# A new job list, new store gates and new planner constants for a convolution followed by a token mixer

## The chip, the cores and the metric

The kernel runs on one core of a Trainium2 chip. The metric is the device time of an execution in microseconds (us), as the median of several runs. The profile is that of a single execution: its span runs from the first to the last instruction, and its own time is a little longer than the span.

## The reference, cut to what matters

```python
# x: 8 x 4224 x 192; weight: 8 x 7; w_q, w_k: 192 x 64; w_out: 192 x 192; all float32
w = softmax(weight)                                  # over the 7 taps, one row per head of 24 channels
y[b, s, head h] = sum_k w[h, k] * x_padded[b, s + k, head h]   # causal, six zeros ahead
wq, wk = y @ w_q, y @ w_k
mixed  = (scale * wq @ wk.T) @ y                     # per batch, scale = 1 / 8
out    = relu(mixed) @ w_out
```

The kernel uses that `wq (wk^T y) = y w_q (w_k^T (y^T y))`. Per batch it forms the 192 x 192 matrix `y^T y`, multiplies it by `w_k` into a 64 x 192 matrix M, and never holds the 4224 x 4224 weights between tokens.

## The kernel before, in words

A batch of 4224 tokens is split into two halves of 2112, and a half into 18 chunks of 122 tokens; a chunk is loaded with the six tokens ahead of it, on 128 partitions, and becomes bf16 in the load. Five batches of x fit in `xw`. The loads of a batch come in two parts (x4.0 is the first part of batch 4, x4.1 the second; batch 1 has four parts and batch 0 eight), all issued from POOL. `y` holds two batches, `qt` two batches, `zt` three blocks of z, and `o_sb` eight blocks of output. PSUM has eight banks: bank 7 keeps the sum of `y^T y`, and banks 0 to 6 go round among the other jobs.

All work is cut into jobs, one letter each in the string `ORDER`:

| letter | job | PE work | evicted or done by |
|---|---|---|---|
| Y | convolution of a group of chunks and heads by a band matrix (L510, L544) | 2 to 8 matmuls, mostly 2 of 128x432 | ACT or DVE to `y` |
| D | copy of the first 64 columns of `y` behind its last, so that windows of 128 wrap | none | DVE, from batch 2 on POOL too |
| T | transpose of three chunks into `yb` (L971) | none | DVE |
| G | one chunk's share of `y^T y` (L644) | 6 matmuls of 128x64 | none |
| E | `y^T y` to `gs` | none | ACT or DVE |
| M | two jobs by turns: a transpose of parts of `gs` into `gt` (L670, L671), and M (L684) | 2 or 6 small matmuls | ACT or DVE to `gt`, `m_sb` |
| Q | half a batch of `w_q^T y^T`, in tiles of 32 rows and 64 columns, on four banks (L614) | 48 matmuls of 32x288 | ACT and DVE to `qt` |
| Z | 512 tokens of a half by 128 columns of `relu(M^T q)` (L720) | 1 matmul of 128x512 | ACT or DVE to `zt` |
| O | output of 512 tokens of both halves in two jobs (L763, L765) | 6 matmuls | ACT or DVE to `o_sb`, then a store from SP |
| A | two Z and one O fused (`fused`): the two Z and O's last part run side by side in tiles of 64 rows (L1127, L1135), then O's other part (L1143) | 2 + 4 + 4 matmuls | as Z and O |
| H, W | zeros ahead of a batch; copies of weights within SBUF | none | DVE, ACT |
| h | names the four banks that the next Q will use and keeps other jobs off them | none | none |

The string is read once while the kernel is built. Each letter takes the next job of its own stream, so the order within a stream is fixed, and the string sets how the streams interleave. PE runs in just this order. For each eviction a planner (`empty`, `pick`, `place`, `fused`) takes the engine that its cost table says will be done first, and the bank that it says will be free first; for that it keeps times of every engine (`COST`, `SWITCH`), of the landing of loads and stores (`flow`, with a rate and latencies in `CLOCK`), and of the fetching of PE's instructions (`stall`, with `CLOCK["fetch"]`: a block of 256 instructions is asked for when the one before it is begun). Where PE would be idle before `CLOCK["fill"]`, it puts in small matmuls on zeros (L1002). None of these times is in the built program: only the orders, engines, banks and fillers that follow from them. The waits of the program are semaphores that come from the data alone.

Stores leave SP in the order of the O jobs; block n is number 5 b + i (i = 4 is the small rest of a batch). `GATES` maps a block to a part of x: the store of this block, and with it all stores behind it on SP, waits until that part has landed. From 4 on the part's number is 2 b + part, so that 8 is x4.0 and 15 is x7.1. A block's slot in `o_sb` is n mod 8, so its eviction waits for the store of block n - 8 to have landed. A load into `xw` waits for the convolutions of the batch five before, and is issued on POOL behind the job D of the batch three before.

Of the kernel before, what the change touches and what calls it, by code (L numbers as in the profile page):

```python
# [11 lines left out]


GATES = {
    0: 8, 3: 9, 5: 10, 10: 12, 15: 14,
}


ORDER = (
    "YYYDYDYDYGTDGGGGYDYYDGTGYYDTGDGGTYTWGGGGGHQGGGTEYYMYDYWMQZZDZZZYYGGZYTGGDGAOTGOT"  # L20
    "YGZZGDOHQGTGYGGYZODOZGYGZGYYGTGGEYYGDMYGGGMTTOGHGAZGYGYYOGTYGGZGZGZQOTGTGYGGYZOG"
    "EDZZYZhGOTGHTMGGDQTMOGZZOYZGZGTZOYTGGZYGGQZGTOQGTZOYYGDZZGZGTYYOGGOEYYGGMOZDHATO"
    "GYOMGZZTGYGGTZOQGZGDOTYGZOOGAZGYGZGZTTGYGQZGOGEAZOGTTGYGMYYGGGGMODhQGZHOGAGGTYYT"
    "GGZOTGQZYGDTGYYOGOGEZZYGDGAMGYTZGGATZOYOHGZGGGTYMQGOZYZGTGYZGATGTGYGZQOOGTAZOGEY"
    "DYGGGYGGGTMAMYOOZZZGGGZDQOTZGOGAOGZTGTGAGGGQGZEOZOMZOZMOZOTZZZOOZOZOQZOZZZOOZZZO"
    "ZOOOO"
)


CLOCK = {  # L30
    "x0": (5.0, 7.5, 9.0, 8.1, 10.2, 12.0, 13.1, 13.8), "band": 6.5, "wq": 14.0, "wk": 16.0,
    "wo": 20.5, "fill": 24.0,
    "dma": (377e3, 13.2, 1.6, {"x": 2.2, "o": 1.2}), "fetch": (64, 256, 5.5, 3.5, 120.0),
}


# [135 lines left out]
def bass_lightweight_conv__then__hypermixer_token_mlp_kernel(  # L172
# [84 lines left out]
    xg = [[P.group(f"x{b}_{g}") for g in range(len(GROUPS[b]))] for b in range(B)]  # L257
# [52 lines left out]
    for g in range(2):  # L310
# [3 lines left out]
            lambda e, g=g, at=(g * HALF + (1 - g) * CW - 6) * D: e.dma_start(  # L314
                staged[g].rearrange("p (c d) -> p c d", d=D),
                bass.AP(x_t, at, [[D, 128], [CW * D, 5], [1, D]]),
            ),
# [104 lines left out]
    band = []  # L422
    for q, eng in enumerate(("act", "dve", "dve", "dve")):
        x0, x1 = (6 if q == 0 else 0), (CW - 90 if q == 3 else 38)
# [37 lines left out]
    wq = [pool(lambda e: e.tensor_copy(WQ[:, :, :], WSQ[:, :, :]), [wl[0]], 0.55)]  # L462
# [143 lines left out]
    def job_q(b, g):  # L606
        def pe(e, bk):
            for j in range(6):
                for i in range(4):
                    r = slice(32 * i, 32 * i + 32)  # L610
                    for h in range(2):
                        c = D * h + 64 * (j // 2) + j % 2
                        rhs = YB[r, g, :, c : c + 63 : 2]
                        last = e.matmul(PS[64 * h : 64 * h + 64, bk + i, 0:288], WQ[r, j, :], rhs,  # L614
                                        start=j == 0, stop=j == 5, skip_group_check=True)
            return last

        evacs = []
        for i0, i1 in ((0, 2), (2, 3), (3, 4)):
            w = 32 if i0 < 3 else CW - 96  # L620

            def make(bk, i0=i0, i1=i1, w=w):
                o = bass.AP(QT, (b % 2) * QW + 9 * CW * g + 32 * i0,
                            [[2 * QW, 128], [32, i1 - i0], [CW, 9], [1, w]])
                i = PS[:, bk + i0 : bk + i1, 0:288].rearrange("p n (c t) -> p n c t", t=32)
                return [(o, i[:, :, :, 0:w])]

            evacs.append((make, ("Q", b, g, i0), (i1 - i0) * 9 * w, "copy"))
        return Job(
            ("Q", b, g), 4, pe, [288] * 6,  # L630
            reads=["wq"] + [("TD", b, 3 * g + k) for k in range(3)],
            after=zdone(b - 2), evacs=evacs, mode="Q",
        )
# [235 lines left out]
    x_at = {}  # L869
# [31 lines left out]

    def land(b, part):
        def f(t):
            x_at[id(xg[b][part])] = t - (b == 1) * (1.0 - 0.8 * (part == 2))
            return x_at[id(xg[b][part])]
        return f

# [72 lines left out]
        return (e.mul(o, i, scale) if eng == "act"  # L980
                else e.tensor_scalar(o, i, scale, None, op0=ALU.mult))

    FIRST, BLOCK, AWAY, NEAR, CALM = CLOCK["fetch"]
    code = [FIRST + 2 * (16 + 1 + 20), 0.0, 0.0]

    def stall(words, t, us):
        at, got = code[0], code[1:]
        to, late = at + words, 0.0
        edge = (at // BLOCK + 1) * BLOCK
        while edge <= to:  # L990
            when = t + us * (edge - at) / words + late
            ok = got[1]
            late += max(0.0, ok - when)
            when = max(ok, when)
            got = [when, when + (AWAY if when < CALM else NEAR)]
            edge += BLOCK
        return late, [to] + got

# [102 lines left out]
    def fused(n):  # L1101
        zs = streams["Z"][head["Z"] : head["Z"] + 2]
        os_ = streams["O"][head["O"] : head["O"] + n]
        b, i = zs[0].name[1:3]
        assert zs[0].name[2:] == (i, 0) and i < 4 and all(j.name[2] < 4 for j in os_)
        at, used, deps, late, t = [], [], [], [], free["pe"]
        for j in (*os_, *zs):
# [3 lines left out]
            t = max(t, free_at + SEE)  # L1111
        for k in used:
            deps += banks[k][1]
        for j in (*zs, *os_):
# [3 lines left out]
            t = max([t] + [o.end + SEE for r in j.reads for o in got(r)])  # L1118
# [27 lines left out]

        pops = []
        for fn, need, m, us, words in (
            (tails, deps, "R", 0.2183 + 0.17 * n, 4 + 8 * n), (heads, late, "F", 0.33 * n, 8 * n),
        ):  # L1150
            o = P.op("pe", fn, need)
            o.start = max(t, free["pe"]) + SWITCH.get((mode[0], m), 0.0)
            mode[0] = m
            wait, code[:] = stall(words, o.start, us)
            total[0] += wait
            o.end = free["pe"] = o.start + us + wait
            o.name = ("R" if m == "R" else "O",) + os_[0].name[1:] + (n,)
            pops.append(o)
# [55 lines left out]
```

## Time and profile before

| | |
|---|---|
| median of 3 runs | 159.13 us (158.52 to 160.15) |
| profiled execution | 158.52 us, span 156.4 us |
| granted TensorE clock | 0.996 |
| PE busy | 137.2 us, 88% of the span |
| ACT busy | 128.4 us, 82% |
| DVE busy | 120.1 us, 77% |
| POOL busy | 58.4 us, 37% |
| HBM read and written | 27.86 MB and 25.95 MB |

Busy time is a share of the whole span, and the span has a start without input and an end in which stores land. A line of groups gives the line, engine, operation, tiles and shape, then the count, the busy time and the mean of one, then the idle time just before them and what ended it. The chain goes from the last instruction back to what released each step; "issue" there is time in which an engine waited for nothing that the profile shows. A window's row has the length, then for each engine its busy time and count, then the granted clock, the DMA share (it can pass 1, since packets overlap on an engine) and the GB/s. The GB/s count a load at its bf16 size, half of what it reads.

### The profile page before, as it was taken

The page shows a single profiled execution, that of the slowest core. Times are in us where ns is not written, and L with a number is a line of the kernel's source. Part 1 is how long each engine was busy: PE and PEld are TensorE (multiplying, and loading weights), DVE is VectorE, ACT ScalarE, POOL GpSimd, SP SyncE. Part 2 cuts the span into 40 slices and gives each one's busy share as a digit, 9 for nine tenths or more (in the row PEclk, how much of TensorE's full clock was granted, in tenths as well). Part 3 has the DMA queues.
Part 4 walks back from the last instruction along what each step waited for, and adds up shares of the span by engine and source line. Part 5 has one row for each costly group of instructions (what it writes and reads, how often), then busy time and mean ns, then how long its engine had stood idle before and what let it go on. Part 6 is the DMA issues. An engine that isn't in the chain of part 4 may idle for free.

```text
span 156.4 us, 5628 instructions
## 1 busy us (share of the span) xinstructions
PE 137.2 (88%) x2431; PEld 101.0 (65%) x2456; DVE 120.1 (77%) x239; ACT 128.4 (82%) x213; POOL 58.4 (37%) x76
## 2 busy tenths in 40 slices
PE   6789758989999999999999999999597999998940
PEld 1367546767777776777777877677374777775720
DVE  6778767949987986888988959899496888795810
ACT  5568559979998899988989988898497888998950
POOL 7999899895764803444200202020020200000000
PEclk9999999999999999999999999999999999999998
DMA  3999999999999999999999999999998556599896
GB/s 100 262 197 182 189 187 187 194 189 193 191 192 192 271 339 340 227 198 341 340 292 192 277 343 337 218 253 394 381 401 323 221 203 235 204 370 395 286 387 225
DMA packets 48441, 40.83 MB, mean 261 GB/s; under 512 B 37281, under 2 KB 40481, under 8 KB 48417
## 3 DMA queue, kind: packets, MB, share of 16 engines
q0 software_dynamic: 36384, 13.35, 72.1%
q1 hardware_dynamic: 12032, 27.14, 47.7%
q8 instruction: 19, 0.31, 0.7%
q14 instruction: 6, 0.04, 0.1%
HBM read 27.86 MB, written 25.95 MB: 344 GB/s over the span
## 4 chain that ended last, share of the span: by engine, by line
PE 72%; POOL 13%; issue 5%; DVE 4%; ACT 2%; ACTq 0%; POOLq 0%
PE ps L644 15%; PE ps L544 12%; PE ps L763 11%; PE ps L765 9%; PE ps L614 8%; POOL xw L280 7%; PE ps L720 6%; PE ps L1143 3%; PE ps L1127 3%; POOL wk L352 1%; PE ps L1135 1%; ACT o_sb L975 1%; PE ps L510 1%; DVE zt L979 1%; POOL xw L297 1%
## 5 line engine op out<-in xcount | busy, mean ns | idle before, releaser
L975 ACT COPY o_sb<-ps 128x768 f32<-128x768 f32 (+1 forms) x61 | 47.2, 787 | 4.7 <-PE ps L765 3.7
L975 ACT CAST y<-ps 128x864 bf16<-128x864 f32 (+6 forms) x47 | 38.1, 833 | 7.8 <-PE ps L544 4.0
L644 PEld LDWEIGHTS ps<-y 128*128 128x128 bf16 (+1 forms) x864 | 35.5, 98 | 12.0 <-issue 2.5
L644 PE MATMUL ps<-y 128*128 128x64 bf16 (+1 forms) x864 | 40.4, 193 | 1.9 <-issue 0.8
L979 DVE TENSOR_SCALAR zt<-ps 128x512 bf16<-128x512 f32 x44 | 29.4, 680 | 8.9 <-PE ps L720 4.4
L975 POOL COPY y<-y 128x1152 bf16<-128x1152 bf16 x11 | 12.6, 1144 | 62.7 <-ACT y L975 41.8
L971 DVE STREAM_TRANSPOSE yb<-y 128x576 int32<-128x576 int32 x48 | 35.6, 758 | 0.1
L763 PE MATMUL ps<-wo,zt 128*128 128x192 bf16 x204 | 33.7, 247 | 1.9 <-ACT o_sb L975 1.2
L765 PE MATMUL ps<-wo,zt 128*128 128x384 bf16 x102 | 33.2, 326 | 0.0
L280 POOL DMA_DIRECT2D xw<-in_x_dram x35 | 32.3, 936 | 2.0 <-POOL xw L439 1.1
L978 ACT ACTIVATE zt<-ps 128x512 bf16<-128x512 f32 x52 | 30.3, 604 | 1.5 <-PE ps L1135 1.1
L763 PEld LDWEIGHTS ps<-wo,zt 128*128 128x128 bf16 x204 | 21.2, 114 | 8.4 <-ACT o_sb L975 1.6
L544 PE MATMUL ps<-xw,band 128*128 128x432 bf16 x96 | 23.9, 346 | 2.2 <-issue 1.8
L975 DVE CAST y<-ps 128x864 bf16<-128x864 f32 (+2 forms) x21 | 21.5, 1026 | 3.9 <-PE ps L544 2.5
L975 DVE CAST qt<-ps 128x288 bf16<-128x288 f32 (+1 forms) x32 | 12.2, 421 | 8.4 <-PE ps L614 8.3
L720 PE MATMUL ps<-qt,m_sb 128*128 128x512 bf16 x45 | 15.3, 380 | 1.8 <-ACT m_sb L980 1.7
L614 PE MATMUL ps<-yb,wq 32*64 32x288 bf16 x768 | 15.7, 284 | 1.0 <-ACT y L975 0.5
L975 ACT CAST qt<-ps 128x576 bf16<-128x576 f32 x16 | 10.2, 640 | 4.4 <-PE ps L614 3.7
L614 PEld LDWEIGHTS ps<-yb,wq 32*64 32x64 bf16 x768 | 10.6, 102 | 2.9 <-issue 1.3
L765 PEld LDWEIGHTS ps<-wo,zt 128*128 128x128 bf16 x102 | 11.6, 113 | 0.0
L544 PEld LDWEIGHTS ps<-xw,band 128*128 128x128 bf16 x96 | 7.4, 98 | 6.1 <-issue 1.9
L510 PE MATMUL ps<-xw,band 128*128 128x120 bf16 (+4 forms) x96 | 8.3, 226 | 2.3 <-DMA xw<-in_x_dram 1.0
(79 smaller groups left out, 121.4 us busy)
## 6 DMA issues: line engine op xcount, KB each, us to landing
out_dram<-o_sb SPq DMA_DIRECT2D x31, 768.0 KB, 7.4
xw<-in_x_dram POOLq DMA_DIRECT2D x14, 432.0 KB, 15.9
xw<-in_x_dram POOLq DMA_DIRECT2D x14, 384.0 KB, 16.9
o_sb<-in_x_dram SPq DMA_DIRECT2D x2, 480.0 KB, 4.5
out_dram<-o_sb SPq DMA_DIRECT2D x16, 48.0 KB, 6.0
out_dram<-o_sb SPq DMA_DIRECT2D x2, 384.0 KB, 3.2
xw<-in_x_dram POOLq DMA_DIRECT2D x2, 240.0 KB, 6.4
xw<-in_x_dram POOLq DMA_DIRECT2D x1, 288.0 KB, 6.9
```

Of the source, the lines that this page charges most:

```text
L280: return e.dma_start(XW[lo:hi, b % NX, half, c : c + n, :], bass.AP(x_t, at, [[D, hi - lo], [CW * D, n], [1, D]]),)
L510: last = e.matmul(PS[:, bk + j // per, at : at + w], BAND[:, h, :], XW[:, b % NX, half, c0:c1, GRP * h : GRP * h + GRP], start=True, stop= ...
L544: last = e.matmul(PS[:, k + j, 0 : 48 * n].rearrange("p (c h d) -> p h c d", h=2, d=GRP), BAND[:, h, :], rhs, start=True, stop=True,)
L614: last = e.matmul(PS[64 * h : 64 * h + 64, bk + i, 0:288], WQ[r, j, :], rhs, start=j == 0, stop=j == 5, skip_group_check=True)
L644: last = e.matmul(PS[:, 7, 64 * k : 64 * k + 64], y[:, 64 * k : 64 * k + 128], y[:, 64 * k : 64 * k + 64], start=c + h + k == 0, stop=c == ...
L720: return e.matmul(PS[:, bk, :], m[:, parts[k] : parts[k] + 128], q, start=True, stop=True)
L763: e.matmul(o[:, 192 * h : 192 * h + 192], z[:, h, cols], WO1[:, :], start=h == 0, stop=False, **kw)
L765: last = e.matmul(o[:, 0:384], z[:, 2, cols], WO2[:, :], start=False, stop=True, **kw)
L971: return e.transpose(o, i)
L975: return e.copy(o, i) if eng == "act" else e.tensor_copy(o, i)
L978: return e.activation(o, i, AF.Relu)
L979: return e.tensor_scalar(o, i, 0.0, None, op0=ALU.max)
```

## The change

The string `ORDER` is replaced, as are the gates and the constants of the planner. The functions keep what they do.

- The number of fused pairs (A) goes from 13 to 3, so Z goes from 78 to 98 letters and O from 59 to 69. The letter h goes from 2 to 5. All other letters keep their number.
- Store 0 waits for x5.0 in place of x4.0; store 8 for x5.1, store 11 for x6.1 and store 18 for x7.1. Before, stores 3, 5, 10 and 15 waited for x4.1, x5.0, x6.0 and x7.0.
- The planner's landing times of the first loads and of `w_out` shift by 0.1 to 2 us. Its time to fetch a block is 7.0 us before 98 us, 8.0 before 121 and 4.8 after, in place of 5.5 before 120 and 3.5 after. A matmul of Q is taken as 292 columns in place of 288, a fused pair as 0.02 us longer.

Counted by form, ACT gets 3 evictions of 128x768 to `o_sb`, 3 of y and one each of `gs` and the small `o_sb` more, 3 of `zt`, both of `gt`, and the five copies of `wk` and `wo` fewer. DVE gets 3 of `zt`, 2 of `gt` and the five copies more, and 3 of `o_sb` and 3 of y fewer. One D moves from DVE to POOL.

```diff
 GATES = {
-    0: 8, 3: 9, 5: 10, 10: 12, 15: 14,
+    0: 10, 8: 11, 11: 13, 18: 15,
 }

 ORDER = (
-    "YYYDYDYDYGTDGGGGYDYYDGTGYYDTGDGGTYTWGGGGGHQGGGTEYYMYDYWMQZZDZZZYYGGZYTGGDGAOTGOT"
-    "YGZZGDOHQGTGYGGYZODOZGYGZGYYGTGGEYYGDMYGGGMTTOGHGAZGYGYYOGTYGGZGZGZQOTGTGYGGYZOG"
-    "EDZZYZhGOTGHTMGGDQTMOGZZOYZGZGTZOYTGGZYGGQZGTOQGTZOYYGDZZGZGTYYOGGOEYYGGMOZDHATO"
-    "GYOMGZZTGYGGTZOQGZGDOTYGZOOGAZGYGZGZTTGYGQZGOGEAZOGTTGYGMYYGGGGMODhQGZHOGAGGTYYT"
-    "GGZOTGQZYGDTGYYOGOGEZZYGDGAMGYTZGGATZOYOHGZGGGTYMQGOZYZGTGYZGATGTGYGZQOOGTAZOGEY"
-    "DYGGGYGGGTMAMYOOZZZGGGZDQOTZGOGAOGZTGTGAGGGQGZEOZOMZOZMOZOTZZZOOZOZOQZOZZZOOZZZO"
-    "ZOOOO"
+    "YYYDYYDYDGGGGYYDTDGYTYGDGTGDTYQYDGGGGGGHTYGTGGGYWYEMDhMQZDZZYZYWYGTDTYGZGZGOYGOO"
+    "DZTTTGGOGGhZhGZGHQGGYZYYGZYGGGDYGOETGGZYTMGTZOGHMGOYYGZGYQGYGDZYTGZZTGYGZGGYGQDG"
+    "ZOTZGYGZOETOOGZYGHGMTZDYQGZTYGOOGOTMOZGGZZTZTYDGhZhQYGGHZYGTYGYGZGOTYZOYGGGEYZDO"
+    "ZOMGOZGGQOZYZGMOTGGYZTYOZGOZZGOGGGDGYGOTGZYYGTGZGGEQOGZGHZOGMGYTOTYZGZGZDYODGMZZ"
+    "TZGGGQGYGZGOZOTOZZZGYYGTGOZOZYOZGGZOTHQZEOTZYYDGYGGZGGTQOGGMZZOYMOGYDGYZOOTZZZOZ"
+    "ZOGGZGGYTGYGOOZTGYOGGEZOGMZZYGDZMGTTOQGTZOGGTGATGOOGGQGZZZTGQZGOAZTOGGGTGGEAMOMZ"
+    "ZOZZZOZOOZOQZOZZZOOZZZOZOOOO"
 )

 CLOCK = {
-    "x0": (5.0, 7.5, 9.0, 8.1, 10.2, 12.0, 13.1, 13.8), "band": 6.5, "wq": 14.0, "wk": 16.0,
-    "wo": 20.5, "fill": 24.0,
-    "dma": (377e3, 13.2, 1.6, {"x": 2.2, "o": 1.2}), "fetch": (64, 256, 5.5, 3.5, 120.0),
+    "x0": (5.0, 7.5, 8.9, 8.1, 10.0, 11.8, 12.8, 13.6), "band": 6.5, "wq": 14.0, "wk": 16.0,
+    "wo": 22.5, "fill": 24.0,
+    "dma": (377e3, 13.2, 1.6, {"x": 2.2, "o": 1.2}), 
+    "fetch": (64, 256, ((98.0, 7.0), (121.0, 8.0), (999.0, 4.8))),
 }
...
-            ("Q", b, g), 4, pe, [288] * 6,
+            ("Q", b, g), 4, pe, [292] * 6,
...
-            x_at[id(xg[b][part])] = t - (b == 1) * (1.0 - 0.8 * (part == 2))
+            x_at[id(xg[b][part])] = t - (b == 1) * (0.3 - 0.1 * (part == 2))
...
-    FIRST, BLOCK, AWAY, NEAR, CALM = CLOCK["fetch"]
+    FIRST, BLOCK, AWAY = CLOCK["fetch"]
...
-            got = [when, when + (AWAY if when < CALM else NEAR)]
+            got = [when, when + next(v for u, v in AWAY if when < u)]
...
-            (tails, deps, "R", 0.2183 + 0.17 * n, 4 + 8 * n), (heads, late, "F", 0.33 * n, 8 * n),
+            (tails, deps, "R", 0.2183 + 0.17 * n, 4 + 8 * n), (heads, late, "F", 0.33 * n + 0.02, 8 * n),
```

## The prediction

> **What bounds the kernel now.** I read the engines' shares first, then the chain, then the waits of PE and of SP's queue.
>
> ```profile
> PE 137.2 (88%) x2431; PEld 101.0 (65%) x2456; DVE 120.1 (77%) x239; ACT 128.4 (82%) x213; POOL 58.4 (37%) x76
> DMA  3999999999999999999999999999998556599896
> q8 instruction: 19, 0.31, 0.7%
> ```
>
> PE is the fullest engine, and in the chain its lines hold 72% of the span. Its idle stretches over 0.15 us add up to 9.0 us, of which 5.1 lie before 23 us; it ends at 150.2, and the last store lands at 155.8. The DMA engines are full until about 118 us, sag, and fill up again. So PE's list, its few waits and the traffic have to be followed together.
>
> ```profile
> PE ps L720 <- ACT m_sb L980: 1.7, 1, 1.7
> PE ps L544 <- issue: 1.8, 2, 1.6
> SPq L164 <- DMA xw<-in_x_dram: 87.6, 5, 44.7
> ...
> 109.75 0.34 PE ps L544
> 110.09 1.62 issue
> 111.71 0.36 PE ps L544
> ```
>
> The first line is the start of Z: `m_sb` is emptied on ACT behind the `wo` copies, which waited 1.0 us for POOL's memset. The second, and the piece of the chain below, is PE standing still with no semaphore behind it, between the two matmuls of one job: it is out of instructions. The third is the gates: SP held its first store until 48.93.
>
> ```profile
> 40.00:48.00 8.00, 7.80 (x161) 5.98 (x162) 6.98 (x13) 7.61 (x14) 6.22 (x7) 1.00 1.60 191
> 53.00:64.00 11.00, 10.40 (x254) 7.86 (x254) 8.32 (x16) 9.93 (x21) 3.94 (x5) 1.00 1.16 332
> 110.00:117.00 7.00, 5.23 (x109) 3.76 (x110) 4.78 (x9) 5.01 (x8) 1.15 (x1) 1.00 1.02 391
> 124.00:130.00 6.00, 5.90 (x111) 4.41 (x113) 4.99 (x11) 5.09 (x10) 0.00 (x0) 1.00 0.38 143
> ...
> DMA to landing us min/median/max: 7.4/7.4/7.4
> DMA to landing us min/median/max: 9.6/10.9/12.2
> ```
>
> The last number of a window is GB/s on the SBUF side. Loads alone: 191, which is 382 read as f32. Loads beside stores: the DMA records of 54 to 60 give 78 read and 302 written, so stores take four fifths. Stores alone: 391. 124 to 130 is nearly idle. The landings are those of the first stores: issued at 48.93, 49.4 and 49.9, landed 7.4, 9.6 and 12.2 us later, so 7.4, 10.1 and 13.2 after the release.
>
> **What the Trainium skill says.** "Runtime: NRT & Kernel Launch", Instruction fetch mechanics: instructions come in 16 KiB blocks of 256, the next one fetched while one is executed, and the cost is "mostly hidden". The 19 packets of 0.31 MB agree with the size; the 1.62 us at 110 are not hidden. "DMA: Bandwidth & Descriptors", Queues, rings and completion order: each engine goes round its queue rows packet by packet, so a fetch queues behind data. The trace agrees: after PE crosses a block's edge, the next fetch packet starts 6.3 us later (from 103.0) and 5.1 (from 111.7) where stores fill the engines, 2.5 (from 127.1) where they are light. "TensorEngine Tiling (Array Packing)", Key Properties: a change of tiling mode drains TensorE; what that leaves of a fused pair's gain is priced below from the chain.
>
> **The change, part by part.**
>
> *Fused pairs, 13 to 3.* In the chain a fused pair takes L1127 0.32, L1135 0.17, L1143 0.46: 0.95. Apart, two Z at 0.215 and one O at 0.65 (L763 0.17, L765 0.16, twice) make 1.08. Ten pairs taken apart: 10 x 0.13 = +1.3 us of PE work. Nothing covers it, PE being the bound: +1.3 (1.0 to 1.6).
>
> *Start of Z.* The `wk` and `wo` copies move from ACT to DVE, `wo` behind the first two relus, and `m_sb` is split over DVE and ACT. So M is emptied soon after its matmul (about 21.8), and Z follows the second Q at about 22.4 in place of 23.88, with one Y (0.37) left for later: -1.1 (0 to -1.6). The last wait there is x's third load, unmoved.
>
> *ACT and DVE.* Counting forms: ACT has 3 more O evictions (0.80), 3 more of Y (0.885), 3 Z fewer (0.604), loses `wk`, `wo` and `gt` copies; in sum about +1.9 us, DVE -1.2. ACT has idle time overall, but is full between 40 and 53 us: +0.4 (0 to 1.9). The dup D(2,0) moves from DVE to POOL, one copy (1.14) ahead of the issue of x5's first half at 35.3; the loads before it are in flight until 53, so that costs nothing unless they finish by 40.
>
> *Gates.* Store 0 waited for x4's first half; now for x5's first half. In before the gates opened at 48.93 (x4.0), 53.22 (x4.1) and 66.34 (x5.0). With no store in between, x5.0's 1.77 MB follow at 382 GB/s: 53.1 + 4.6 = 57.8. Stores 0, 1, 2 then land at 57.8 + 7.4, 10.1, 13.2 = 65.2, 67.9, 71.0. There are eight `o_sb` slots, so O(1,3), O(1,4), O(2,0) need just these. Where is PE then? Add up PE durations in list order (G 0.175, Y 0.365, Q 1.36 with both switches, Z 0.215, O 0.65). In before O(1,3) is complete at 51.4 of that sum and at 64.5 in the chain: an offset of 13.1, and still 13.2 at the eighth Q (77.0). With the early 1.1 won, after has 12.0. O(1,3)'s first half, at 52.8, is ready at 64.8, O(1,4) at 55.7 at 67.7: both at their limit. O(2,0), at 56.6, is ready at 68.6 and waits until 71.0, on ACT. Behind it on ACT stand its second half and Q(3,1)'s eviction; Q(3,1)'s four banks include O(2,0)'s two. So Q starts at 71.0 + 0.05 + 0.80 = 71.9 and not at 58.0 + 12.0 = 70.0: +1.9 (0 to 3.5). In before O(2,0) came at 55.2 + 13.1 = 68.3 and its slot was free at 62.1: 6 us in hand, now none. If the early 1.1 isn't won, this wait is 1.1 shorter: the two share one fate, and sum to +0.8 either way.
>
> *Blocks of code.* 256 instructions are 128 matmuls. In before the block from 103.0 holds 6.9 us of PE work and its fetch took until 111.7: 8.7. In after the blocks there hold 8.9 and 8.5: the 1.62 goes, -1.6 (0 to -1.6). The wait at 118.4 (0.87, PE for an `o_sb` eviction just behind a fused pair) goes with the pair: -0.9 (0 to -0.9). But then come blocks of 5.4 and 6.2 us. The 5.4 starts at 110.4 of the sum, about 123.5. In before that stretch was light: from 127.1 the packet ended at 130.55, and with the 1.45 seen at 110 between packet and matmul a block took 4.9. Is it still light? Stores 0 to 10 (7.3 MB at 302) hold the engines from 61.8 to 86, x6.1 lands near 90, stores 11 to 17 follow from 94 to 110 beside x7.1, which lands near 110; only then is store 18 let go (gate 18 on x7.1, before 15 on x7.0). From 114 stores 18 to 26, 5.7 MB at 391, hold the engines until about 128.6. So the fetch from 123.5 meets full engines, as that from 111.7 did: 5.1 + 0.95 + 1.45 = 7.5 against 5.4: +2.1 (0 to 3.3).
>
> *Sum* against the profiled execution (158.52, span 156.4, 2.1 around it): +1.3 - 1.1 + 0.4 + 1.9 - 1.6 - 0.9 + 2.1 = +2.1, so 160.6. That execution was the lowest of the three shown; the median is 0.6 above it: 161.2. I say **161.1**.
>
> **Rivals.**
>
> *A, both new waits stay out; faster.* If the stores land 2.4 us sooner than I place them, or O(2,0) comes as much later, no slot is missed; and if the backlog of stores is gone by 124, no block is late. Then +1.3 - 1.1 + 0.4 - 1.6 - 0.9 = -1.9: 157.2. For it: two of the three slots are met to 0.4 us, and from 23 to 109 us PE had only 0.8 us of idle stretches, so the list's dependencies are sound. Against it: the landings are measured, and the slot's slack fell from 6 us to nothing. It decides at a landing of store 2 before 69 us.
>
> *B, one of the two comes; no change.* With the slot wait alone 159.1, with the block alone 159.3.
>
> *C, waits multiply; clearly slower.* Eight stores are now let go at once, and gate 11 on x6.1 puts store 11's landing at 97.5 against O(3,4)'s need of it at 86.8 + 13.5 = 100.3. If stores squeeze x6.1 by 5 us more, O(3,4) and O(4,0) wait 2 to 3 us, ACT's queue with them: 163.5 to 165.
>
> *D, nothing moves, since the new constants issue no instruction.* Not so: they choose engines, banks and filler matmuls (11 to 8, all before 15 us, where PE waits for x anyway: 0), the two lists part at the sixth letter, and the gates move.
>
> **How the numbers follow.** Forecast 0.45 (160.0 to 162.5), C 0.15, B 0.24 (158 to 160), A 0.16. Range: from A's middle, 157.2, to the lower part of C, 164.2. A change of 1% is about what a measurement of this kernel can tell from none: 157.5 and 160.7. Faster takes most of A, 0.13; same is B with the slow end of A and the quick end of the forecast, 0.29; slower 0.58.
>
> **What would show it.** Right: SP's first store near 57.8 and an ACT `o_sb` eviction near 69 to 71 ended by the DMA of `out_dram`; PE idle before an L615 at about 70; Z at 22.4; no issue gap near 110, one of about 2 us near 129. Wrong: the first store before 55, no wait on `out_dram`, gaps elsewhere (a DVE or ACT queue that runs late), or PE waiting for `xw`.

## The result, and the profile after

| | before | after |
|---|---|---|
| median of all executions, us | 157.93 (47) | 157.26 (42) |
| lowest to highest, us | 154.83 to 160.15 | 156.38 to 159.15 |
| profiled execution, us (its span) | 158.52 (156.4) | 157.10 (155.2) |
| TensorE ends, us | 150.2 | 149.2 |

The ratio of after to before is 1.0087, 95% interval 1.0063 to 1.0112. The prediction was 161.1, slower by more than 1%. The comparison takes only the executions within 1.5% of a kernel's fastest, so the ratio sets after against before at its best (up to 157.2); over all executions after's median is 0.7 us *lower*. Both are true because before's executions are spread over 5.3 us and after's over 2.8. By the 1% bound this is no difference. What has to be explained is why two kernels with quite different lists come out alike, and why one scatters and the other doesn't.

The page of after: engines, DMA slices, the queue of code packets.

```profile
PE 139.0 (90%) x2405; PEld 101.6 (65%) x2433; DVE 117.5 (76%) x240; ACT 128.8 (83%) x211; POOL 59.5 (38%) x77
DMA  3999999999999999999999999999359999689896
q8 instruction: 19, 0.31, 0.7%
```

The waits of after: engine, operation and line, what it waited for, us in total, times, longest. The third line is that of 60 to 74 us alone.

```profile
PE ps L615 <- issue: 1.0, 1, 1.0
ACT o_sb L976 <- DMA out_dram<-o_sb: 0.8, 1, 0.8
...
PE ps L615 <- ACT o_sb L976: 0.2, 1, 0.2
...
PE ps L721 <- ACT m_sb L981: 0.4, 1, 0.4
...
SPq L804 <- DMA xw<-in_x_dram: 53.7, 1, 53.7
```

The windows of after: busy us of PE, PEld, DVE, ACT and POOL, then clock, DMA share and GB/s.

```profile
53.00:64.00 11.00, 10.34 (x213) 7.44 (x214) 8.22 (x19) 10.96 (x20) 3.77 (x6) 1.00 1.51 223
108.00:114.00 6.00, 5.89 (x70) 4.19 (x71) 4.20 (x9) 5.78 (x12) 1.15 (x1) 1.00 0.30 95
122.00:130.00 8.00, 7.90 (x199) 6.25 (x200) 6.93 (x15) 7.08 (x15) 0.00 (x0) 1.00 1.03 387
```

The stores of after that were issued from 57 to 60 us, the first three:

```profile
DMA to landing us min/median/max: 7.2/10.3/12.4
```

PE is busy 1.8 us longer than before and still ends 1.1 us earlier. The first store goes out at 57.91 (predicted 57.8); stores 0, 1 and 2 land at 65.07, 68.69 and 71.28 (predicted 65.2, 67.9, 71.0). The DMA engines are nearly idle between 108 and 114 (a share of 0.30) and full from 122 to 130, as worked out. The slot wait is there, 0.8 us on ACT, and behind it PE stands before an L615, but for 0.17 us only, at 72.30. Near 129 it crosses the edge of a block in a step of 0.10, which is what such a step takes elsewhere too. Instead it stands here, in the chain at 46 to 49 us (start, us, what):

```profile
46.96 0.26 PE ps L615 x8
47.22 0.98 issue
48.20 0.81 PE ps L615 x30
```

That is a wait for code in a stretch for which the prediction had none.

**Counting the edges.** Count every instruction of TensorE in program order (a weight load and its matmul are two); each 256 make a block. Where does PE stand when it crosses a block's edge, and how long before had the last code packet ended? The phase of the count was set once, by the pause at 110 in before, and kept for every kernel; the number of edges is then that of the code packets, 19. From the traces of the two kernels, at the edges with a pause that is not an ordinary step:

```
before: edge   32.54->33.36  54.09->54.35  60.62->61.38  95.72->95.95  109.72->111.71  118.14->119.25
        pause  0.82          0.26          0.76          0.23          1.99            1.11           sum 5.2
        last packet ended before:  1.62  1.27  1.59  1.35  1.44  1.59
after:  edge   17.88->18.81  46.91->48.20
        pause  0.93          1.29                                                                     sum 2.2
        last packet ended before:  1.38  1.45
```

At all eight the packet had ended 1.27 to 1.62 us before PE went on; at the other edges 1.8 to 6.1 (but for the first edge of each, and one at 1.33 with nothing lost). So in these traces a block was not used sooner than some 1.3 to 1.6 us after its packet had ended, and PE stood where it came to the edge before that. A pause is given here, and below, as the whole step between two weight loads; in profiles without the pause these steps take 0.02 to 0.33, so some 4.6 us are lost in before and 2.1 in after. The prediction saw one of before's six (the one at 110), and put the one at 118 down to an eviction.

### The profile page after: what moved, and what is told of

Same layout as the page of the kernel before. It is cut to its first block, busy times and chain, and to the rows that moved or that the text cites. A ratio compares the mean times of both kernels' runs of the same rounds, so it can differ in the third digit from the quotient of the medians.

```text
span 155.2 us, 5566 instructions
## 1 busy us (share of the span) xinstructions
PE 139.0 (90%) x2405; PEld 101.6 (65%) x2433; DVE 117.5 (76%) x240; ACT 128.8 (83%) x211; POOL 59.5 (38%) x77
## 4 chain that ended last, share of the span: by engine, by line
PE 69%; DMA 12%; ACT 5%; issue 3%; DVE 3%; POOL 3%; ACTq 0%; POOLq 0%
PE ps L645 14%; PE ps L764 12%; PE ps L766 11%; PE ps L545 9%; PE ps L721 8%; PE ps L615 8%; DMA out_dram<-o_sb 8%; DMA xw<-in_x_dram 4%; PE ps L511 3%; POOL xw L281 2%; ACT y L976 2%; ACT o_sb L976 2%; DVE qt L976 2%; DVE yb L972 1%; PE ps L1144 1%
## 5 line engine op out<-in xcount | busy, mean ns | idle before, releaser
L976 ACT COPY o_sb<-ps 128x768 f32<-128x768 f32 (+1 forms) x65 | 49.6, 788 | 4.9 <-PE ps L766 3.0
L976 ACT CAST y<-ps 128x864 bf16<-128x864 f32 (+6 forms) x50 | 40.9, 838 | 5.1 <-PE ps L511 4.1
L764 PE MATMUL ps<-wo,zt 128*128 128x192 bf16 x244 | 40.4, 247 | 0.4 <-ACT o_sb L976 0.3
L766 PE MATMUL ps<-wo,zt 128*128 128x384 bf16 x122 | 39.8, 326 | 0.0
L980 DVE TENSOR_SCALAR zt<-ps 128x512 bf16<-128x512 f32 x47 | 31.6, 686 | 8.1 <-PE ps L766 3.6
L764 PEld LDWEIGHTS ps<-wo,zt 128*128 128x128 bf16 x244 | 25.0, 115 | 8.1 <-ACT o_sb L976 0.7
L721 PE MATMUL ps<-qt,m_sb 128*128 128x512 bf16 x62 | 21.1, 380 | 0.6 <-ACT m_sb L981 0.4
L976 DVE CAST y<-ps 128x864 bf16<-128x864 f32 (+2 forms) x18 | 18.2, 1017 | 3.3 <-PE ps L545 2.1
L615 PE MATMUL ps<-yb,wq 32*64 32x288 bf16 x768 | 15.4, 284 | 3.3 <-DVE yb L972 1.4
L976 ACT CAST qt<-ps 128x576 bf16<-128x576 f32 (+1 forms) x17 | 10.5, 625 | 7.9 <-PE ps L615 7.5
L615 PEld LDWEIGHTS ps<-yb,wq 32*64 32x64 bf16 x768 | 10.6, 102 | 5.8 <-issue 1.9
L766 PEld LDWEIGHTS ps<-wo,zt 128*128 128x128 bf16 x122 | 13.8, 113 | 0.0
L721 PEld LDWEIGHTS ps<-qt,m_sb 128*128 128x128 bf16 x90 | 8.1, 97 | 3.7 <-DVE m_sb L982 0.7
```

The source lines that it names most:

```text
L721: return e.matmul(PS[:, bk, :], m[:, parts[k] : parts[k] + 128], q, start=True, stop=True)
L764: e.matmul(o[:, 192 * h : 192 * h + 192], z[:, h, cols], WO1[:, :], start=h == 0, stop=False, **kw)
L766: last = e.matmul(o[:, 0:384], z[:, 2, cols], WO2[:, :], start=False, stop=True, **kw)
L976: return e.copy(o, i) if eng == "act" else e.tensor_copy(o, i)
L980: return e.tensor_scalar(o, i, 0.0, None, op0=ALU.max)
```

## The experiments

The theory formed here: before has less work for TensorE but waits for code, by an amount that changes from one execution to the next; the change adds work (the pairs) and takes waits away, and the two cancel. The rivals: the prediction's own account (slot waits from the gates, an eviction at 118), and that a new order and plan simply fall out this way. "Plan unchanged" below means: the planner still sees the old list and gates, so every engine keeps its instructions and their order.

**Before again.**

> The kernel before, unchanged, for a second profile of it. My prediction stands on one profile of it, with an issue gap of 1.62 us at 110 and a wait of 0.87 us at 118. If these belong to the list (theory 1), they stand at the same places again. If they are accidents of that execution (theory 2), this profile lacks them, PE ends 1.5 to 3 us earlier, and what I booked as won by leaving them out (2.5 us) was never there to win. The ratio must be 1.00.

157.56 (155.18 to 161.56, 14 executions), beside it before at 158.21 (155.63 to 159.73, 19); ratio 0.998, 0.992 to 1.004. The spread is the kernel's. The pauses lie at the same edges with other sizes: 0.76, 0.53, 0.53, 0.23, 1.44 and 1.67.

**Ten pairs apart, the list rewritten and replanned.**

```diff
-...TGGDGAOTGOT
+...TGGDGZZOOTGOT      (the first ten A become ZZO)
```

> The list of before with its first ten letters A written as ZZO, so that three fused pairs are left, as in the changed kernel; gates and constants as before. If PE's work sets the end (theory 1), it is 10 x 0.13 = 1.3 us slower, ratio 1.008. If the fused pairs' drain and their joint wait for z and banks cost as much as they save (rival), within 0.4 us of before.

162.91; ratio 1.0385, 1.0296 to 1.0474. The fetch pauses are nearly gone (0.3 in all), but the weight loads now wait 2.6 us for `yb`, and PE up to 1.0 at a time for `o_sb` and 1.4 for `zt`: other evictions went to other engines. It measures the replanning along with the pairs and decides nothing; so did the next two.

**The gates exchanged, replanned.**

```diff
-GATES = {0: 8, 3: 9, 5: 10, 10: 12, 15: 14}
+GATES = {0: 10, 8: 11, 11: 13, 18: 15}
```

> The list and constants of before, with the changed gates alone. Store 2 lands near 71 in place of 62. The list has its ninth to eleventh output blocks at 62.3 to 68.3, so if a missed slot stops ACT and then PE, as my prediction has it, this one loses 2 to 4 us near 65 to 71 and the ratio is 1.013 to 1.025. If the slot wait is soaked up by free banks, under 1 us: 1.000 to 1.006.

158.66; ratio 1.011, 1.0036 to 1.0183. ACT waits three times, 5.1 us in sum, for a store to leave its slot, PE stands 1.27, 0.58 and 0.38 at 63 to 72; the pauses at 110 and 118 are gone.

> The changed list and constants, with the gates of before. The first store is let go at 49 in place of 58. If the new gates cost the changed kernel time by slots (theory 1), it is up to 1 us faster than the changed kernel: ratio to before 1.002. If they cost nothing, 1.009 as the changed kernel. If the loads of x5 to x7, later by up to 9 us under the old gates, are now late for the changed list's earlier Y jobs, slower than the changed kernel: 1.015 or more, with PE or DVE waiting for xw.

After with before's gates: 160.96; ratio 1.0281, 1.0183 to 1.0379. From 60 us on evictions are spread differently over DVE and ACT, and the loss lies there.

**The gates exchanged, plan unchanged.** Only the wait that SP issues is taken from another table:

```diff
+HOLD = {0: 10, 8: 11, 11: 13, 18: 15}
-            gate = GATES.get(n, -1)
+            gate = HOLD.get(n, -1)
```

> The kernel before with its own plan (engines, banks, fillers unchanged), and only the stores held by the changed gates, so that the gates act without the new plan that they brought in the run with new gates. Theory F (fetching of PE's code is what the list of before waits for, and it depends on traffic): the pauses at the edges of the blocks near 110 and 118, 3.1 us in two profiles, vanish since no store runs from 110 to 114; slot waits of 2 to 3 us near 65 to 71 come in; about as before, ratio 0.995 to 1.015, with a narrow spread of times. Rival S (the slots are soaked up): 2.5 us faster than before, 0.985. Rival (the pauses belong to the list, whatever the traffic): slower by the slots, 1.02.

158.52; ratio 1.0122, 1.0058 to 1.0187. Its chain, at 58 to 66 us, is the predicted mechanism:

```profile
57.81 7.14 DMA out_dram<-o_sb
...
65.02 0.81 ACT o_sb L978
65.83 0.05 issue
65.88 0.35 PE ps L766 x2
```

Store 0 lands, its slot is free, the eviction follows, then PE, which had stood 1.39 us. So late gates do make a slot wait that reaches PE, in before's list. The pauses near 110 and 118 are gone in this execution.

> The kernel before with its own plan, the first three gates as before, and the last two as in the changed kernel: store 11 waits for x6.1 and store 18 for x7.1, in place of store 10 for x6.0 and 15 for x7.0. Theory F: no slot is missed, and the fetch pauses near 110 and 118 go: 2 to 3 us faster than the profiled before, PE ends near 147.5, ratio of medians 0.985. If fetching isn't the cause, the pauses stay and the ratio is 1.00; if x7 comes late, PE waits for xw and it is slower.

With `HOLD = {0: 8, 3: 9, 5: 10, 11: 13, 18: 15}` (the first three gates as before, the later two as in after): 157.66 (22 executions); ratio 1.0077, 1.0023 to 1.013. A slot wait of 0.9 us is there, on DVE, and PE stands 0.22 for it, at 101.8. The 0.985 that was expected did not come: the median is close to that of before beside it, 157.89. But its profiled execution (156.34) is one without fetch pauses, and so it settles the wait at 118. Weight loads of PE (start, us), in before and in this kernel, and ACT's queue in this kernel:

```profile
118.14 0.10 PEld L720 LDWEIGHTS ps<-qt,m_sb 128*128 128x128 bf16 x1
119.25 0.33 PEld L763 LDWEIGHTS ps<-wo,zt 128*128 128x128 bf16 x2 [1.02 <-ACT o_sb L975]
```

```profile
117.03 0.10 PEld L723 LDWEIGHTS ps<-qt,m_sb 128*128 128x128 bf16 x1
117.11 0.33 PEld L766 LDWEIGHTS ps<-wo,zt 128*128 128x128 bf16 x2
...
117.35 0.80 ACT L978 COPY o_sb<-ps 128x768 f32<-128x768 f32 x1
```

The eviction that before's trace names as the releaser, and that ended at 119.26 there, begins in this kernel 0.24 us *after* the load it is said to hold up. The load never needed it, nor did its matmul, which starts at 117.49, before the eviction ends. In before 118 is a block's edge, and the eviction merely ended at the same time as the pause.

> The changed kernel with its own plan, its stores held only by the gates of before. In the run with old gates the plan changed from 60 us on as well, and it lost 3.6 us. If the old gates themselves cost that (later loads of x5 to x7, or fetch pauses), it is 2 to 4 us slower than the changed kernel, with waits for xw or pauses at block edges from 100 us on; if it was the plan, it is within 0.7 us of the changed kernel.

After, plan unchanged, with before's gates: 158.16; ratio 1.0101, 1.0027 to 1.0175, so no better than after. A different wait is there, on DVE at 65.93:

```profile
65.93 0.14 DVE L977 MEMSET xw<- 6x96 uint32 x1 [2.13 <-DMA xw<-in_x_dram]
```

A load that shares the engines with earlier stores comes late, and PE loses 1.1 us behind it. For after's list the new gates cost 0.8 us on ACT, 0.17 on PE, and save this.

**The pairs kept, their work made longer.**

```diff
-  M_SB[rows, ...], QT[rows, ...]; z[rows, 2, cols[r]] x WO2S[rows, :]
+  M_SB[:, ...],    QT[:, ...];    z[:, 2, cols[r]]    x WO2[:, 192*h : 192*h+192]
```

> The kernel before with its own plan and order, and only the fused pairs' first part issued over all 128 rows, one after another, in place of two tiles of 64 rows side by side: the same number of instructions, evictions and waits, no change of tiling mode, so it is the pair's saving alone. If PE's work is the bound, 13 x 0.13 = 1.7 us slower by my price, 13 x 0.21 = 2.7 us by the steps between matmuls in the traces of this case. Theory F: part of it is soaked up by the fetch pauses (5 us in the profile), which shrink as PE is slower: 0.5 to 1.5 us slower in the median.

The two Z and the tails of all 13 pairs go over 128 rows instead of twice 64, the number of instructions stays: 160.08; ratio 1.0212, 1.0137 to 1.0287. That is 2.2 above before beside it, more than the 0.5 to 1.5 expected. The pauses at 110 and 118 are gone here too (0.20 and 0.08), which fits that the next block has come when the same code takes more time; one of 0.71 at 62 is left.

**The edges moved.** At the very start, warm-up matmuls are cut into smaller ones of the same total width: 64 more matmuls, 128 more instructions, ahead of all else.

```diff
-                o = e.matmul(PS[:, 0, :], WARM[:, 0:128], WARM[:, :], start=True, stop=True)
+                k = small.pop() if small else 1
+                for j in range(k):
+                    o = e.matmul(PS[:, 0, 0 : 512 // k], WARM[:, 0:128], WARM[:, 0 : 512 // k], ...)
```

> Before, with ten of the warm-up matmuls at the very start cut into smaller ones of the same total width: 64 matmuls, that is 128 instructions, more ahead of everything else, and no other difference. Every edge of 256 instructions comes half a block earlier in the work. Theory (the waits that have no late operand are waits for the next block of code): the steps at which TensorE stood before (near 32.5, 60.6, 110 and 118) go through within 0.3 us, and whatever pauses there are now lie at the new edges, halfway between the old ones; their sum may be smaller or larger, so the median may lie anywhere from 155.5 to 160. Rival (the waits belong to those steps: an output slot or a PSUM bank that is emptied late): TensorE still stands near 110 and near 118 for 1 to 2 us, median 157.9.

158.99 (157.79 to 159.95); ratio 1.0168, 1.0131 to 1.0205. Its chain:

```profile
64.06 0.16 PE ps L649 x2
64.23 1.09 issue
65.31 0.29 PE ps L649 x4
...
100.81 1.06 issue
101.87 0.35 PE ps L649 x6
```

The pauses are now 1.31 (at 22.76), 1.30 (65.31), 0.44 (94.14) and 1.38 (101.86), every one at a *new* edge, in the middle of jobs that ran through before, with the last packet ended 1.28 to 1.47 us earlier. The steps at which before stood go through (now at 34.4, 55.1, 62.0, 97.8 and 119.7) with no more than the 0.33 that the one at 62.0 takes anyway; the one at 112.9 waits 0.38 for an operand. This shows that the pauses belong to the code's position and not to the work.

**Ten pairs apart, plan unchanged.** This is the main part of the change, alone: only the emission differs, 8 matmuls in place of 10.

```diff
+        apart = pairs_done[0] < 10
...
+                if apart:
+                    e.matmul(PS[:, za[h], :], M_SB[:, ...], QT[:, ...], start=True, stop=True)
...
+                        e.matmul(PS[:, bk + r, 192 * h : 192 * h + 192], z[:, h, cols[r]], WO1[:, :], ...)
+                    e.matmul(PS[:, bk + r, 0:384], z[:, 2, cols[r]], WO2[:, :], ...)
```

> The list, the gates and the plan (which engine empties what, in which order) stay those of before; only the first ten fused pairs issue their two Z and one O as separate matmuls, 8 instead of 10 each. That is the main part of the change done alone. Theory (a fused pair saves TensorE 0.21 us, and its denser code is what the code fetch can't follow): TensorE's work grows by 10 x 0.21 = 2.1, the pauses at the edges of 256 instructions fall from the 5.2 of the profiled execution to under 1.5, the two long ones (2.0 near 110, 1.1 near 118) are gone; median 157 to 158.5, and the executions lie within about 3 us of each other instead of 5. Rival 1 (the pairs cost 0.13 each and have nothing to do with the pauses): 159.2, pauses near 110 and 118 as before, executions 5 us apart. Rival 2 (issuing apart is itself dear, as the replanned run suggested): 162 to 163.

158.35 (156.71 to 159.70, but for one execution of 488 us, which was also the profiled one); ratio 1.0109, 1.0044 to 1.0173.

> The kernel with before's first ten pairs issued apart, plan unchanged, once more: its profiled execution was a disturbed one of 488 us, so where its pauses lie is not known. Theory: against the profiled execution of before, ten pairs cost 0.21 each (+2.1 on TensorE), the pauses at the edges of 256 instructions fall from 5.2 to under 2, none over 0.6 near 110 and 118; median 157.5 to 158.5, executions within 3.5. Rival (the pauses stay, and the earlier median was luck): over 4 us of pauses, median 159.5 or more.

157.96 (156.40 to 159.89, 20 executions), with before beside it at 157.96 (154.84 to 160.99, 54); ratio 1.0117, 1.0077 to 1.0156. So the median does not move, and the spread falls from 6.1 to 3.5. The ratio sets it against before at its best, and there it is 1.8 us slower. The pauses sum to about 3.5 in the profiled execution, not "under 2", and one of 1.03 is left at 113. Load by load against before, a pair taken apart delays what follows by 0.147 us in seven of the ten, by 0.17, 0.24 and 0.35 in the others: 1.8 in all. That is neither the 0.13 of the prediction nor the 0.21 of these expectations. It does not reach the median, and the trace shows one way in which it is made good: before the edge at 33 the list is 0.2 us behind before's, and behind it 0.6 ahead, since before had stood there for code.

**After, with five pairs fused again,** at places where two Z and an O stand together.

```diff
-...YOZGOZZGOGGG...   ...ZZZOZOGG...   ...MZZOZZZOZOOZOQZOZZZOOZZZOZOOOO
+...YOZGAGOGGG...     ...ZZAZOGG...    ...MZZAZOZOOZOQZAZOOZAZOOOO
```

> After, with five pairs of the list fused again where two Z and an O of one row block are neighbours, at 78 us and later; the planner's choice of engines stays the same but for a few evictions. Theory (a pair saves 0.21, and after has 2 us or more in hand at its edges from 55 us on): 5 x 0.21 = 1.05 less than after, 156.2, with executions still within 3 us. Rival 1 (the price is 0.13): 156.6. Rival 2 (the fetch pauses come back with the pairs): at or above after's 157.3, with a pause of 0.5 or more at one of the last edges and executions further apart.

161.24; ratio 1.0241, 1.0148 to 1.0334: 3.5 slower than after beside it (157.79). No theory had it. The plan is made anew here; a few evictions change places, one small one its engine. One new pause for code is large (1.01 at 131.2), and there is a new wait ahead of the fused pairs:

```profile
PEld ps L1128 <- ACT o_sb L976: 1.9, 2, 1.1
```

A pair asks for its four PSUM banks at once, two of them just being emptied. At three of the five places the list falls 0.46 to 0.54 us behind across the pair, where a gain was expected. But another 1.2 us are lost between 80 and 105.5, where no pair stands, in waits for evictions. So this run does not tell what a pair alone costs in after's list.

**After again.**

> After, unchanged, on the same chip as the other three, to compare them with it. Theory: median 157.3 within 0.4, executions within 3 us of each other, where before's scatter over 5; the median of before on this chip within 0.7 of after's, and the same early pauses (near 18 and near 47).

157.79 (156.32 to 159.56, but for one of 238 us), before beside it 158.25; ratio 1.0103, 1.0057 to 1.0149. The early pauses are the same (0.93 and 1.29), and this execution has the one near 129:

```profile
128.69 0.38 PE ps L615 x15
129.08 0.60 issue
129.68 0.70 PE ps L615 x31
```

At that edge the step takes 1.00 us (0.10 in the first profile). The request after the edge at 123.9 came 3.34 us later here, 1.90 there.

**The start alone, in three ways.** A second difference between executions had come up by now. In four profiles of before's list (both with the gates held at plan unchanged, the one with longer pairs, the one with moved edges) the clock is down just after the idle stretch at 22 to 24; in the windows (22 to 26 and 26 to 28 us) of the run with the two late gates, and below them in the first window of before's own profile:

```profile
22.00:26.00 4.00, 2.55 (x23) 0.98 (x8) 1.73 (x5) 3.50 (x9) 3.65 (x7) 0.73 1.53 181
26.00:28.00 2.00, 2.00 (x24) 1.69 (x23) 1.26 (x2) 1.11 (x3) 2.00 (x3) 0.70 1.60 192
...
22.00:26.00 4.00, 2.33 (x41) 1.47 (x26) 2.47 (x6) 3.78 (x10) 3.65 (x7) 1.00 1.57 185
```

The 0.73 and 0.70 are means: a window from 23.9 to 27.1 us has a clock of 0.50. A 512-column Z takes 0.43 us there in place of 0.22, and by 28 us the four are 1.6 to 1.8 us behind before. Of this 0.8 comes back at 33, where before's profile stands 0.82 for code and these go through. In before's own profile and in after's the clock of these windows is 1.00, though before's idle stretch ahead of Z, 1.67 us, is no shorter than theirs (0.7 to 1.6). Of 177 executions of before that stood beside the experiments, 47 have a mean clock under 0.985; their median is 158.83, that of the other 130 is 157.53. With a full clock before's median is thus only 0.5 below the 157.99 of all 177. Of 64 of after none has; but of the 18 executions of after's list with other gates or more pairs four have, and in their profiles the stretch is filled as in after's.

> Before with 12 more matmuls in its warm-up at the start (four of its wide ones cut into 16 of the same total width): all edges of 256 instructions come 24 instructions earlier in the work. From the pauses-free timeline of before and the delays of the code packets seen in all profiles so far (request 1 to 6 us after an edge by stretch, 0.95 for the packet, 1.4 until it can be used) the pauses should come to 1.8 on average in place of 3.1. Theory: median 156.8, 1.1 less than before's, the clock lists as mixed as before's (a quarter of the executions at 0.984 or lower). Rival (where the edges lie changes the places but not the sum): 158.

Twelve more matmuls at the start: 158.26, but only 6 executions, one at 154.36 and five at 157.5 to 158.8, so no interval was had. The profiled one has about 6 us of pauses. Where the edges lie did not lower the sum as I had reckoned.

```diff
+            if job.name == ("Z", 0, 0, 0):
+                ...
+                fill(k, 12, banks[k][1])
```

> Before with the same 12 more matmuls, now full warm-up matmuls of 256 columns issued just ahead of the first Z, where TensorE stands for about 1.5 us at 22 to 24. The edges after it lie as in the run with 12 more at the start. Theory (the low clock of 0.6 to 0.8 that some profiles of before's list show from 24 to 27.6, and that cost 1.6 to 1.9 us in them, comes from that idle stretch): no execution under 0.985, no lower clock at 24 to 28, and the median 0.4 less than that of the run with 12 more at the start, 156.4, with executions within 4. Rival (the lower clock has nothing to do with the idle stretch): a quarter of the executions at 0.984 or lower, median 156.8.

The same twelve in the idle stretch ahead of the first Z: 155.64 (154.30 to 157.96, 22 executions); ratio 0.992, 0.9883 to 0.9957. No clock under 0.988. The times lie in two groups, 14 at 154.3 to 156.0 and 8 at 157.0 to 158.0; the profiled one is of the upper group and has pauses at most edges.

```diff
-    "wo": 20.5, "fill": 24.0,
+    "wo": 22.5, "fill": 24.0,
```

> Before with one of the change's constants alone: the due time of w_out 22.5 in place of 20.5. The planner then puts M's evictions ahead of the second w_out copy and seven warm-up matmuls ahead of Z, so that Z starts earlier and the idle stretch at 22 is filled; the edges move by 14 instructions. Theory: Z starts near 22.6 in place of 23.7, no execution under 0.985; 0.5 to 1.1 of it reaches the end where pauses do not take it back; median 156.6 to 157.4. Rival (the early start only meets the code fetch sooner): 158, and the pauses are larger by as much as Z started earlier.

One of the change's constants alone. It makes the planner give one `wo` copy and half of M's eviction to DVE and one part of `qt` to ACT, and put seven warm-up matmuls into the gap; at 81 us a Y and a Z exchange their engines too: 155.19 (154.97 to 157.65, 17 executions), 2.8 below before beside it; ratio against before at its best 0.9975, 0.9939 to 1.0012. Z starts only 0.1 us earlier and not at 22.6 as expected, so it is not the start that pays. Its pauses are 0.84 and 0.40 and little else; at 109.4 and 116, before's two long ones, PE takes 0.03 and 0.08.

> Before with the due time of w_out at 22.5 alone, once more, on the same chip as the run with the pairs apart. Theory: median 155.2 within 0.4, most executions within 1 of each other, none under a clock of 0.985, and below both before (157.9) and after (157.3). Rival (the first run of it was luck): 156.5 or more, as scattered as before.

155.34 (154.72 to 156.66, 22 executions), before beside it 157.58; ratio 0.9965, 0.9934 to 0.9995. It repeats, and it is below both kernels. Two of its 22 executions do have a low clock (0.983 and 0.971, at 156.19 and 156.66), which I had excluded. Its profiled execution, one of its longest (156.17), has pauses of 0.81, 0.58, 0.63 and 0.48.

> Before with the due time of w_out at 22.5 (as in the run that gave 155.2) and, besides, its first ten pairs issued apart, plan otherwise unchanged: the two parts of the change that the runs so far point to, together. Theory (the pairs cost 10 x 0.21 of TensorE's work where the pauses are already small, and their work was hidden in pauses only where those were large): 155.2 + 2.1 less at most 1 of the remaining pauses, 156.3 to 157.3, near after's 157.3, executions within 3. Rival (pairs issued apart are free, as they were in before): 155.2.

The same constant, and ten pairs apart: 158.03 (157.63 to 158.80); ratio 1.0192, 1.0136 to 1.0248. That is 2.7 above the constant alone, and above both expectations, where before's ten pairs apart cost nothing in the median. The pairs' own work is 1.8 of it. The profiled execution has pauses of 0.58, 0.59, 0.60 and 0.39, some 0.9 more than the first one of the constant alone, so here the pauses did not shrink; each is one execution.

**Put together.** Before 157.9; with the start's constant 155.2 to 155.3; with the pairs apart 158.0; with both 158.0; after, with these and a new order and gates, 157.3 to 157.8. So the constant and the pairs, the two parts tested together, about cancel, and 0.2 to 0.8 are left for the order, the gates and the rest. Pairs taken apart cost TensorE 1.8. That in before part of it is paid for by shorter pauses, and that all of it is paid where code is in time, fits these runs but is argued from single profiles. The change's own constants fit it too: they give a block 7.0 and 8.0 us to come, where before's gave 5.5; in the traces 3.5 to 5, 0.95 for the packet and 1.3 to 1.6 make 5.8 to 7.5. So the new list was laid out against longer waits for code, and has fewer of them: 2.2 and 3.2 in its two profiled executions, in place of 5.2 in both of before's.

## Why the prediction was wrong

The prediction's sum was right about what the change issues and wrong about where TensorE stands still. By its own steps, in the profiled executions:

| step | predicted, us | shown, us |
|---|---|---|
| fused pairs | +1.3 | +1.8, measured in before's list |
| start of Z | -1.1 | -0.9: 1.2 earlier, one Y of 0.37 left for later |
| ACT and DVE | +0.4 | +0.5 |
| gates | +1.9 | +0.2 |
| pauses at 110 and 118 | -1.6, -0.9 | -2.0, -1.0 |
| block near 129 | +2.1 | 0 |
| pauses at other edges after Z's start | nothing | -1.6 (four in before), +1.2 (46.9 in after) |
| sum | +2.1 | -1.8 |

The two executions differ by -1.4 (158.52 and 157.10), so 0.4 stays open. **The steps that failed are the two new waits, of the gates and of the block near 129, and the pauses for code at other edges, which were put at nothing.**

- *Gates, +1.9.* The times of the stores were right to 0.8 us, and the mechanism is shown in before's list (1.39 us at 64.5). What failed is the place of PE: Q was to be ready at 70.0, and PE came to it at 72.13. On its way lie the pause at 46.9, which takes 1.2, and five waits of 0.16 to 0.33 for evictions and a memset between 33 and 64 us, 1.1 together. So ACT's wait of 0.8 left 0.17 for PE, and in the second profile of after there is no slot wait at all. The step also left out what the late gates save: with the old ones, DVE waits 2.13 us for a load and PE 1.1.
- *Blocks of code, -1.6 and -0.9 and +2.1.* The pause at 110 went, as said. The wait at 118 went too, but for another reason: it was code, and the trace's releaser a coincidence. The stall near 129 came in one of two profiles of after: a step of 1.00 in the second, no pause in the first, 2.1 predicted. The block there holds 4.8 us of work, not 5.4, and the request took 1.9 to 3.3 us, not the 5.1 carried over from 111.7: a delay seen once was taken as a constant. "Runtime: NRT & Kernel Launch", Instruction fetch mechanics, of the Trainium skill says that the crossing costs one tail bump of a DMA, mostly hidden. In these traces it is 0 to 2 us each and up to about 5 us an execution.
- *Fused pairs, +1.3.* The sign was right and the size is 1.8 with the plan unchanged, since three of the ten places cost 0.17 to 0.35. But "nothing covers it" failed: in before's list the median does not move. "PE being the bound" was read from 88% busy, and at six edges the bound was the code.
- *Start of Z, -1.1.* Z's first matmul starts at 22.66, after an idle of 0.42, in place of 23.88; its first weight load starts at 22.41. What filling the idle stretch brings is more than the early start, and not in the prediction: the constant alone, with Z only 0.1 earlier, lowered the median by 2.2 to 2.8. The low clock is at most a small part of that, since before's executions with a full clock have a median of 157.53. The rest is not explained: the same twelve matmuls gave 158.26 at the start, with no low clock in six executions, and 155.64 in the gap.
- *ACT and DVE, +0.4.* From 24 us on PE waits 1.4 us for evictions in after and 0.9 in before, in stretches of over 0.12. That is the size foreseen; it was not tested by itself.
- *Sum against one execution.* The prediction took the profiled execution's 158.52 for what before needs, and the median of three, 159.13. That execution had 5.2 us of pauses in it, the median of 47 is 157.93, and 10 of the 47 need under 156.

Its rival A gave the number, 157.2, and that is luck. By its own test, a landing of store 2 before 69 us, it was out (71.28): the waits stayed small because PE came later. And it counted a gain of 1.9 from a median of 159.13, where the medians differ by 0.7.

Open: what sets, from one execution to the next, how long a code request waits (1.9 or 3.3 us at one edge of after, 5.9 or 6.3 at one of before); what the constant's gain of 2.2 to 2.8 us consists of; why executions of one kernel fall into groups; and whether the idle stretch *causes* the low clock: after idles 1.4 us at 14 and shows none, and before's own profile idles 1.67 at 22 and shows none. The new order itself, without gates and pairs, was not tried.

## What to carry to other kernels

Before costing an edit, count the instructions of the fullest engine and mark every 256th: a step that stands still there, with the last code packet ended less than some 1.7 us before, waited for code in these traces, whatever releaser they named, and fewer busy microseconds on that engine can then be worth nothing. Look at the spread of the executions before trusting one profile; two kernels with the same median can differ in what holds them. And change an order with the plan held fixed when asking what a part of it costs, for a replanned list moves the losses elsewhere.

## What the runs showed of the hardware

- At the pauses a block of 256 instructions was used 1.27 to 1.7 us after its packet ended; from the edge to the start of the next packet it was 0.1 to 6.3 us, mostly 3.5 to 5 while loads or stores fill the DMA engines, and in after at the same edge 1.9 in one execution and 3.3 in another.
- Moving all edges by 128 instructions moved the pauses: 1.31, 1.30, 0.44 and 1.38 us at new edges, and none left at the old places.
- A fused pair gained 0.147 us over two Z and one O issued apart at seven of ten places; the chain's pieces had suggested 0.13.
- TensorE's clock was 0.50 for 3.4 us after an idle stretch of 0.7 to 1.6 us at 22 in four profiles, and 1.6 to 1.8 us were lost; after 1.67 us at the same place in before's profile it stayed at 1.00.
- Ten pairs apart cost 0 or 2.7 us in the median, in two lists that differ by one constant of the start. That lateness of code decides it is not shown by itself.
